# A transformer block on one core: the V products of two token blocks moved ahead of the first q and k products

## The chip, the core and the metric

The kernel runs on one core of a Trainium2 chip. PE is TensorE (matmuls and transposes), DVE is VectorE, ACT is ScalarE, POOL is GpSimd, and SP only issues DMAs here. PEld is the loading of a matmul's stationary operand. The metric is the device time of one execution in microseconds (us).

## The reference

The input is x, 2048 tokens of 512 numbers, all float32. It is normalized (mean 0, variance 1 over the 512, epsilon 1e-5). The result feeds two branches whose product is added to x:

```python
xn = layernorm(x)
q, k, v = split(xn @ wqkv)            # 32 heads of 16
s = concat(softmax(q @ k.T / 4) @ v) @ wo
g = silu(gelu(xn @ w1 + b1) @ w2 + b2)   # 1376 hidden
out = x + s * g
```

## The kernel before

**Precision.** A matmul operand is split in two parts: a high part, rounded on ACT, and a low part, the rest, computed on DVE or POOL (`split`, L86 and L87, for the normalized x; `w_split`, L294 and L295, for weights). A product then is three matmuls: high by high, high by low and low by high (`mm3`, L92).

**Blocks and chunks.** The tokens are worked in 16 blocks of 128, and four blocks make a chunk of 512. `xh` and `xl` hold the transposed high and low parts of a chunk.

**The first stage.** `load_x` fetches a block (L405). `ln` works on four blocks: statistics and their aggregate on DVE (L414, L415), one root for all four (L419 to L424: five small DVE operations with a square root on ACT, L420, between the first two), then four norms (L428). `turn` transposes a block on PE (L437) and splits it. `q_first` makes q and k of the first two head groups for a chunk: 24 matmuls of 512 columns (L455). Its `evac` copies the two results on ACT (L370), rounds them (L374), takes the low parts on POOL (L375), and SP stores the four tiles in DRAM (L380, L381). `v_tile` makes V of one block: 12 matmuls (L92), copied out on ACT (L387). V's own weights come in four pieces (L469), whose high parts are rounded on ACT (L511) and whose low parts are made on POOL (`wv_low`, L502). `pool_after(t)` is a one-element POOL operation that reads the norm of block t, so POOL does nothing that follows it before that norm is done. `keep_warm` issues small matmuls whose result nobody reads (L487).

On PE the first stage goes: warm-up matmuls, transposes of chunk 0, `q_first(0)`, transposes of chunk 1, V of block 0, `q_first(1)`, transposes of chunk 2, V of block 1, `q_first(2)`, transposes of chunk 3, V of block 2, `q_first(3)`, V of block 3.

**What follows.** When chunk 3 is transposed, the first stage's memory is given up. SP then issues `load_qs(0)`, six loads of q rows from DRAM (L146), and `load_k(0, ...)`, six loads of k rows of the first 512 tokens (L121); these come behind the stores of `q_first(2)` in SP's queue. The next stage is a list of products with 64 rows on each half of the PE array ("row tiles" 0 and 1): first V of blocks 4 to 15, four blocks at a time (`quad`, L583), then the feed-forward branch and the remaining q and k. Between these products, one after about five, stand the scans: a matmul of q and k rows (`s_mm`, L193) whose row maximum DVE takes (`s_max`, L199). The first scan stands behind the first four matmuls of the first quad. It needs the q and k rows of row tile 0, the second scan those of row tile 1. Later stages compute the scores again, with exponentials and V, and the output product.

**What sets the order.** The schedule is manual: every engine executes its instructions in the order in which the code issues them, and semaphores hold an instruction until what it reads is there. Nothing behind a held instruction of an engine is executed before it.

Of the kernel before, what the change touches and what calls it, by code (L numbers as in the profile page):

```python
# [8 lines left out]
F32 = mybir.dt.float32  # L9
F32R = mybir.dt.float32r  # L10
AF = mybir.ActivationFunctionType
# [5 lines left out]
P = 128  # L17
# [32 lines left out]
XB = 6  # L50
# [4 lines left out]
def fused(ctx: ExitStack, tc: tile.TileContext, x, wqk, wv, wo, w1, b1, w2, b2, out):  # L55
# [333 lines left out]
    with ExitStack() as s1:  # L389
# [19 lines left out]
        mv = wp.tile([P, NT, 2], F32, name="mv")  # L409
        ve = wp.tile([P, 5, NT], F32, name="ve")  # L410

        def moments(t):
            st = w1k.tile([P, 6], F32, name="st")
            nc.vector.bn_stats(st, xs[t])  # L414
            nc.vector.bn_aggr(mv[:, t, :], st)  # L415

        def rstd(t0, t1):
            v = ve[:, :, t0:t1]
            nc.vector.tensor_scalar(v[:, 0], mv[:, t0:t1, 1], EPS, None, op0=OP.add)  # L419
            nc.scalar.activation(v[:, 1], v[:, 0], AF.Sqrt)  # L420
            nc.vector.reciprocal(v[:, 2], v[:, 1])
            nc.vector.scalar_tensor_tensor(v[:, 3], v[:, 2], -0.5, v[:, 2], op0=OP.mult, op1=OP.mult)
            nc.vector.tensor_mul(v[:, 3], v[:, 3], v[:, 0])
# [9 lines left out]
        def turn(t):  # L433
            pt = a_tile((P, KT, P))
            xn = xns.pop(t)
            for k in range(KT):
                nc.tensor.transpose(pt[:, k, :], xn[:, k * P:(k + 1) * P], ident)  # L437
            c, ts = t // NCH, slice(t % NCH * P, t % NCH * P + P)
            split(xh[c][:, :, ts], xl[c][:, :, ts], pt)
# [5 lines left out]
                mm3(pv, (xh[c][:, k, ts], xl[c][:, k, ts]), (wv_h[:, k], wv_l[:, k]), k == 0, k == KT - 1)  # L445
            v_out(t, pv)

        def q_first(c):
            pq = {}
            for n, (i, j) in enumerate(((0, 0), (0, 1), (1, 0))):  # L450
                for g in range(2):
                    if n == 0:
                        pq["q", g, c] = a_tile((P, CH))
                    for k in range(KT):
                        nc.tensor.matmul(pq["q", g, c], W1[g][i][:, k * P:(k + 1) * P], (xh, xl)[j][c][:, k],  # L455
                                         start=n == 0 and k == 0, stop=n == 2 and k == KT - 1)
            evac(list(pq), pq)

        for t in range(4):
            load_x(t, (nc.sync, nc.scalar)[t % 2])  # L460
        warm = wp.tile([1, 2], F32, name="warm")
        nc.vector.memset(warm, 1.0)
        nc.scalar.activation(warm[:, 1:], warm[:, :1], AF.Sqrt)
        for g in range(2):
            W1[g] = w_new(wqk[:, g], 2, "raw1")
        for t in range(4, 6):
            load_x(t)
        for k in range(KT):
            nc.sync.dma_start(wv_r[:, k], wv[:, k])  # L469
        for t in range(6, XB):  # L470
# [14 lines left out]
        def keep_warm(n):  # L485
            for _ in range(n):
                nc.tensor.matmul(pw[:, :P], ident, ident, start=True, stop=True)  # L487

        keep_warm(25)
        def ln(t, n):  # L490
            for i in range(t, t + n):
                moments(i)
            rstd(t, t + n)
            for i in range(t, t + n):
                norm(i)

        ln(0, NCH)
        def pool_after(t):
            nc.gpsimd.tensor_sub(warm[:, :1], xns[t][:1, :1], xns[t][:1, :1])

        def wv_low(k):
            nc.gpsimd.tensor_sub(wv_l[:, k], wv_r[:, k], wv_h[:, k].bitcast(F32))  # L502

        pool_after(NCH - 1)
        for g in range(2):
            W1[g] = w_split(W1[g], "w1", 4)
        for t in range(NCH):
            turn(t)
        keep_warm(3)
        for k in range(KT):  # L510
            nc.scalar.activation(wv_h[:, k], wv_r[:, k], AF.Copy)  # L511
        for k in range(KT - 2):
            wv_low(k)
        ln(NCH, NCH)
        consts()
        pool_after(2 * NCH - 1)
        for k in range(KT - 2, KT):
            wv_low(k)
        q_first(0)
        for c in range(1, NCH):  # L520
            for t in range(NCH * c, NCH * c + NCH):
                turn(t)
            if c < NCH - 1:
                ln(NCH * c + NCH, NCH)
            else:
                nc.scalar.activation(warm[:, 1:], warm[:, :1], AF.Gelu_apprx_tanh)
                break
# [553 lines left out]
```

## Time and profile before

| | us |
|---|---|
| timed runs, median of 3 | 1547.04 (1546.8 to 1547.23) |
| span of the profiled execution | 1544.6 |
| PE busy in it | 1538.4 (100%) |
| DVE busy | 1419.2 (92%) |
| ACT busy | 1212.4 (78%) |
| POOL busy | 375.8 (24%) |

The profile shows one execution, whose span runs from the first to the last instruction; the timed runs lie 2.4 us above it. PE's busy time is modelled with matmuls that overlap, so 100% says that PE always has a matmul under way and not that it is at its peak. Times in rows count from the span's start. In a row such as `9.13 1.11 PE L437 ... x8 [0.22 <-DVE xn L428]` a group of 8 instructions starts at 9.13 and takes 1.11 us to the end of the last, and PE sat idle for 0.22 us before it until DVE's L428 was done. An fp32 transpose or warm-up matmul leaves two records. SPq is SP's queue, PEldq PE's sequencer, which goes ahead of the array and waits on semaphores.

### The profile page before, as it was taken

Reading aid. Unit: us, or ns where it says so; the run is one execution under the profiler, and the core shown is the slowest. Engines: PE = TensorE matmul, PEld = TensorE weight load, DVE = VectorE, ACT = ScalarE, POOL = GpSimd, SP = SyncE. Lnnn points to the kernel's source line nnn. Section 1 sums busy time; section 2 is a strip of 40 time slices with the busy share of each in tenths; the row PEclk is TensorE's granted clock in tenths of the full one; section 3 lists DMA queues with packets and bytes.
Section 4 is the critical chain, followed back from the end, with each engine's and each line's share of the span. In section 5 each row is a group of like instructions: output and inputs, shape, how many; then the busy total and the mean of one; then the engine's idle time right before and its main releaser. Section 6 shows DMA issues by size and latency. Waiting matters only on the chain.

```text
span 1544.6 us, 31302 instructions
## 1 busy us (share of the span) xinstructions
PE 1538.4 (100%) x12230; PEld 922.5 (60%) x12230; DVE 1419.2 (92%) x2294; ACT 1212.4 (78%) x1881; POOL 375.8 (24%) x386
## 2 busy tenths in 40 slices
PE   9999999999999999999999999999999999999998
PEld 8899999999995444444444444444444444444456
DVE  7799999999998999999999999999999999999945
ACT  4333433333339999999999999999999999999994
POOL 4235575756741011001000100100010000000153
PEclk9999999999999999999999999999999999999999
DMA  6615443455422112112411411411051111110162
GB/s 212 155 58 145 124 143 108 120 161 136 141 90 66 39 45 61 33 37 51 75 28 33 71 33 41 60 44 29 21 84 29 32 32 30 41 32 20 50 217 100
DMA packets 78227, 116.83 MB, mean 76 GB/s; under 512 B 28132, under 2 KB 28388, under 8 KB 76904
## 3 DMA queue, kind: packets, MB, share of 16 engines
q1 hardware_dynamic: 73596, 99.80, 23.1%
q0 software_dynamic: 4000, 14.45, 5.0%
q8 instruction: 96, 1.57, 0.4%
q10 hardware_dynamic: 484, 0.60, 0.1%
q14 instruction: 51, 0.42, 0.1%
HBM read 84.35 MB, written 25.97 MB: 71 GB/s over the span
## 4 chain that ended last, share of the span: by engine, by line
PE 99%; DVE 1%; DMA 0%; issue 0%; ACT 0%; DVEq 0%
PE pv L787 33%; PE ps L193 22%; PE ps L583 13%; PE two L716 8%; PE sp L583 5%; PE ps L716 4%; PE pst L716 4%; PE pst L583 3%; PE pv L583 2%; PE ps L916 2%; PE ps L92 1%; PE ps L455 1%; PE pst L92 0%; DVE st L414 0%; PE two L92 0%; DMA xt<-in_x 0%
## 5 line engine op out<-in xcount | busy, mean ns | idle before, releaser
L199 DVE TENSOR_REDUCE mx<-ps 128x2 f32<-128x512 f32 x2048 | 1318.0, 687 | 68.5 <-PE ps L193 18.3
L787 PE MATMUL pv<-slot,vsb 128*32 128x512 f32 x4096 | 543.4, 604 | 0.0
L721 ACT ACTIVATE slot<-two 128x1024 f32<-128x1024 f32 x511 | 520.5, 1019 | 0.0
L193 PEld LDWEIGHTS ps<-kt,slot 48*128 48x128 f32 x1356 | 212.2, 184 | 290.2 <-DVE mx L199 278.4
L193 PE MATMUL ps<-kt,slot 48*128 48x256 f32 (+1 forms) x1356 | 376.3, 366 | 0.0
L719 ACT ACTIVATE slot<-ps 128x512 f32<-128x512 f32 x515 | 307.5, 598 | 16.7 <-PE ps L716 7.2
L719 ACT ACTIVATE slot<-pst 128x512 f32<-128x512 f32 x511 | 309.9, 606 | 0.0
L583 PE MATMUL ps<-slot,w1h 64*128 64x512 f32 x1088 | 225.4, 392 | 0.0
L193 PE MATMUL ps<-kt,qz 48*128 48x512 f32 x512 | 202.2, 395 | 0.0
L716 PE MATMUL two<-qt,kt 50*128 50x512 f32 x766 | 197.5, 395 | 0.3 <-DVE gt L643 0.3
L716 PE MATMUL ps<-qt,kt 50*128 50x512 f32 x387 | 189.7, 492 | 0.0
L193 PEld LDWEIGHTS ps<-slot,slot 48*128 48x128 f32 x590 | 92.8, 184 | 124.0 <-DVE mx L199 118.2
L193 PE MATMUL ps<-slot,slot 48*128 48x256 f32 (+1 forms) x590 | 165.8, 366 | 0.0
L787 PEld LDWEIGHTS pv<-slot,vsb 128*32 128x32 f32 x4096 | 81.5, 108 | 131.9 <-issue 124.4
L583 PEld LDWEIGHTS ps<-slot,w1h 64*128 64x128 f32 x1088 | 154.1, 185 | 9.8
L583 PE MATMUL ps<-slot,w1l 64*128 64x512 f32 x544 | 157.0, 392 | 0.0
L716 PE MATMUL pst<-qt,kt 50*128 50x512 f32 x383 | 155.7, 406 | 0.0
L375 POOL TENSOR_TENSOR hl<-hg,hh 128x512 fp32r<-128x512 f32 x76 | 96.7, 1295 | 158.2 <-ACT hh L374 109.3
L368 ACT ACTIVATE hg<-ps,b_sb 128x512 f32<-128x512 f32 x44 | 27.9, 684 | 133.0 <-PE ps L583 121.7
L716 PEld LDWEIGHTS two<-qt,kt 50*128 50x128 f32 x766 | 114.5, 186 | 1.1 <-DVE gt L643 0.7
L246 POOL CAST mh<-nt 128x32 fp32r<-128x32 f32 x19 | 4.0, 209 | 375.7 <-DVE nt L244 322.8
L193 PEld LDWEIGHTS ps<-kt,qz 48*128 48x128 f32 x512 | 93.7, 183 | 1.0 <-DVE mx L199 0.7
(197 smaller groups left out, 1974.6 us busy)
## 6 DMA issues: line engine op xcount, KB each, us to landing
raw<-in_w SPq DMA_DIRECT2D x88, 256.0 KB
qk_h<-hh SPq DMA_DIRECT2D x32, 256.0 KB
qk_l<-hl SPq DMA_DIRECT2D x32, 256.0 KB
qt<-qk_h SPq DMA_DIRECT2D x128, 64.0 KB
slot<-qk_h SPq DMA_DIRECT2D x92, 64.0 KB
g_d<-gt POOLq DMA_DIRECT2D x16, 256.0 KB, 3.3
qt<-qk_l SPq DMA_DIRECT2D x64, 64.0 KB
dn<-den_d SPq DMA_DIRECT2D x32, 128.0 KB
```

Source lines behind the costliest of these rows:

```text
L92: nc.tensor.matmul(ps, lhs[a], rhs[b], start=first and n == 0, stop=last and n == 2)
L193: return nc.tensor.matmul(ps[:, c0:c0 + w], QS[u][r, p, qi * P:(qi + 1) * P], kts[u // NCH % KB][p][r, k0:k0 + w], start=True, stop=True).ins
L199: nc.vector.tensor_reduce(MX[u][:, 2 * p:2 * p + 2, qi, ki][:, heads, parts], ps.rearrange("p (n c) -> p n c", c=HC), axis=AX.X, op=OP.max)
L368: nc.scalar.activation(raw, ph.pop(u), AF.Gelu_apprx_tanh, bias=b1_sb[:, u[2]:u[2] + 1])
L375: nc.gpsimd.tensor_sub(hl, raw, hh.bitcast(F32))
L455: nc.tensor.matmul(pq["q", g, c], W1[g][i][:, k * P:(k + 1) * P], (xh, xl)[j][c][:, k], start=n == 0 and k == 0, stop=n == 2 and k == KT - 1)
L583: i = nc.tensor.matmul(ps, lhs[r], rhs[r], start=first, stop=last).ins
L716: nc.tensor.matmul(ps, kts[g % KB][p][r, k * P:(k + 1) * P], QT[u][r, p, :], start=True, stop=True)
L719: nc.scalar.activation(PT[u, k][:, 2 * p + a, :], ps, AF.Exp, scale=SCALE)
L721: nc.scalar.activation(PT[u, k][:, :2], TP["two"], AF.Exp, scale=SCALE)
L787: nc.tensor.matmul(PV[u][32 * j:32 * j + 32, :], vsb[:, k, h:h + 32], PT[u, k][:, j, :], start=(k == 0), stop=(k == NT - 1))
L916: HALF[0] = nc.tensor.matmul(PW[i][0], OTS[i, k][x][r], (wo_h, wo_l)[y][r, k], start=k == 0 and side == 0 and n == 0, stop=k == KT - 1 and ...
```

## The change

Six things change in the first stage.

- Block 0 is fetched in two halves by SP's and ACT's queues, block 1 by SP, block 2 by ACT, block 3 by SP. The V weights come ahead of the q and k weights, with block 3 behind their second piece.
- Blocks 0 and 1 get a square root of their own, and so do blocks 2 and 3. The root adds epsilon on ACT (`eps` is a small tile), so DVE has four small operations after it and none before.
- ACT rounds three pieces of the V weights ahead of the split of block 0, and the fourth ahead of the split of block 1. POOL makes the low parts of two pieces behind the norm of block 1 and of two behind the norm of block 3, and only then those of the q and k weights.
- The V products of blocks 0 and 1 are made ahead of `q_first(0)`, term by term (`v_term`), with the transposes of blocks 2 and 3 between them.
- The V products of blocks 2 and 3 take the places that those of blocks 0 and 1 had. Nothing stands any more between the transposes of chunk 3, `q_first(3)` and the first quad.
- The transposes of chunk 3 stand inside `q_first(2)`, ahead of its last four matmuls. The load of the Gelu table (`warm`, last line) comes behind the evacuation of `q_first(2)`. There are 15 warm-up matmuls instead of 28.

```diff
+        def root(t0, t1):
+            nc.scalar.activation(ve[:, 1, t0:t1], mv[:, t0:t1, 1], AF.Sqrt, bias=eps)
         def rstd(t0, t1):
-            nc.vector.tensor_scalar(v[:, 0], mv[:, t0:t1, 1], EPS, None, op0=OP.add)
-            nc.scalar.activation(v[:, 1], v[:, 0], AF.Sqrt)
...
+        def v_term(t, n):
+            i, j = ((0, 0), (1, 0), (0, 1))[n]
+            if n == 0:
+                VP[t] = a_tile((P, D))
+            c, ts = t // NCH, slice(t % NCH * P, t % NCH * P + P)
+            for k in range(KT):
+                nc.tensor.matmul(VP[t], (xh, xl)[i][c][:, k, ts], (wv_h, wv_l)[j][:, k],
+                                 start=n == 0 and k == 0, stop=n == 2 and k == KT - 1)
+            if n == 2:
+                v_out(t, VP.pop(t))
+
-        def q_first(c):
+        def q_first(c, mid=()):
...
+                    if n == 2 and g == 1:
+                        for t in mid:
+                            turn(t)
...
-        for t in range(4):
-            load_x(t, (nc.sync, nc.scalar)[t % 2])
+        xs[0] = w1k.tile([P, D], F32, name="xt", bufs=XB)
+        for eng, r in ((nc.sync, slice(0, P // 2)), (nc.scalar, slice(P // 2, P))):
+            eng.dma_start(xs[0][r], x[r, :])
+        load_x(1)
+        load_x(2, nc.scalar)
...
+        for k in range(KT):
+            if k == 2:
+                load_x(3)
+            nc.sync.dma_start(wv_r[:, k], wv[:, k])
         for g in range(2):
             W1[g] = w_new(wqk[:, g], 2, "raw1")
...
-        keep_warm(25)
+        keep_warm(15)
...
+        moments(0)
+        moments(1)
+        root(0, 2)
+        stats(2)
+        rstd(0, 2)
+        norm(0)
+        norm(1)
+        aggr(2)
+        moments(3)
+        for k in range(KT - 1):
+            wv_high(k)
+        pool_after(1)
+        turn(0)
+        wv_high(KT - 1)
+        turn(1)
+        root(2, 4)
+        rstd(2, 4)
+        norm(2)
+        norm(3)
+        for k in range(2):
+            wv_low(k)
+        pool_after(3)
+        for k in range(2, KT):
+            wv_low(k)
         for g in range(2):
             W1[g] = w_split(W1[g], "w1", 4)
+        v_term(0, 0)
+        v_term(1, 0)
+        v_term(0, 1)
+        turn(2)
+        v_term(1, 1)
+        turn(3)
+        v_term(0, 2)
+        v_term(1, 2)
         ln(NCH, NCH)
...
-        for c in range(1, NCH):
+        for c in range(1, NCH - 1):
             for t in range(NCH * c, NCH * c + NCH):
                 turn(t)
...
-            v_tile(c - 1)
-            q_first(c)
+            ln(NCH * c + NCH, NCH)
+            v_tile(c + 1)
+            q_first(c, range(NT - NCH, NT) if c == NCH - 2 else ())
+        nc.scalar.activation(warm[:, 1:], warm[:, :1], AF.Gelu_apprx_tanh)
...
     load_k(0, c0=CH, n=S - 2 * CH)
-    v_tile(NCH - 2)
     q_first(NCH - 1)
-    v_tile(NCH - 1)
     load_k(0, c0=S - CH, n=CH)
```

The change shifts line numbers: transposes are L446, the early V products L465, `q_first` L480, warm-up matmuls L517, V weight roundings L533, low parts L536, quads L633.

How instructions move on PE at the start. Before (`slot_97` and `slot_101` are `xh` and `xl` of chunk 0, `kt_113` holds the V weights' parts, `w1h` and `w1l` those of q and k):

```order
L487 MATMUL pv<-ident 128x128 x25
L437 MATMUL ps<-ident,xn 128x128 x8
L437 MATMUL sp<-ident,xn 128x128 x8
L487 MATMUL pv<-ident 128x128 x3
L455 MATMUL pst<-slot_97,w1h 128x512 x4
L455 MATMUL ps<-slot_97,w1h 128x512 x4
L455 MATMUL pst<-slot_101,w1h 128x512 x4
```

With the change:

```order
L517 MATMUL pv<-ident 128x128 x15
L446 MATMUL ps<-ident,xn 128x128 x8
L465 MATMUL sp<-kt_113,slot_97 128x512 x8
L465 MATMUL sp<-kt_113,slot_101 128x512 x4
L446 MATMUL pst<-ident,xn 128x128 x4
L465 MATMUL sp<-kt_113,slot_101 128x512 x4
L446 MATMUL ps<-ident,xn 128x128 x4
L465 MATMUL sp<-kt_113,slot_97 128x512 x8
L480 MATMUL ps<-slot_97,w1h 128x512 x8
```

24 V matmuls and the transposes of blocks 2 and 3 now stand between the first two blocks' transposes and `q_first(0)`.

On ACT at the start, before (L420 is the root, L294 rounds the q and k weights, L86 is a block's split, L511 rounds the V weights):

```order
L420 ACTIVATE ve<-ve 128x4
L294 ACTIVATE w1h<-raw_135 128x512
L294 ACTIVATE w1h<-raw_137 128x512
L86 ACTIVATE slot_97<-ps 128x4x128 x2
L86 ACTIVATE slot_97<-sp 128x4x128 x2
L511 ACTIVATE kt_113<-wv_r 128x512 x4
```

With the change (L426 is the root, L533 rounds the V weights):

```order
L426 ACTIVATE ve<-mv,eps 128x2
L533 ACTIVATE kt_113<-wv_r 128x512 x3
L86 ACTIVATE slot_97<-ps 128x4x128
L533 ACTIVATE kt_113<-wv_r 128x512
L86 ACTIVATE slot_97<-ps 128x4x128
L426 ACTIVATE ve<-mv,eps 128x2
L294 ACTIVATE w1h<-raw_142 128x512
```

Three weight roundings now stand ahead of block 0's split.

On PE at the third `q_first` (chunk 2 is `slot_99` and `slot_103`, chunk 3 `slot_100` and `slot_104`), before; V of block 2 follows with 12 matmuls of L92, of which the first rows are shown, then the last `q_first`, V of block 3 with 12 more, four quad matmuls and the first scan:

```order
L455 MATMUL ps<-slot_103,w1h 128x512 x8
L455 MATMUL ps<-slot_99,w1l 128x512 x8
L437 MATMUL sp<-ident,xn 128x128 x8
L437 MATMUL pst<-ident,xn 128x128 x4
L437 MATMUL ps<-ident,xn 128x128 x4
L92 MATMUL ps<-kt_113,slot_97 128x512 x2
L92 MATMUL ps<-kt_113,slot_101 128x512
```

With the change, from there to the first scan L193:

```order
L480 MATMUL sp<-slot_99,w1l 128x512 x4
L446 MATMUL pst<-ident,xn 128x128 x4
L446 MATMUL ps<-ident,xn 128x128 x12
L480 MATMUL sp<-slot_99,w1l 128x512 x4
L480 MATMUL sp<-slot_100,w1h 128x512 x8
L480 MATMUL sp<-slot_104,w1h 128x512 x8
L480 MATMUL sp<-slot_100,w1l 128x512 x8
L633 MATMUL pst<-kt_113,slot_98 128x512
L633 MATMUL pv<-kt_113,slot_98 128x512
L633 MATMUL pst<-kt_113,slot_98 128x512
L633 MATMUL pv<-kt_113,slot_98 128x512
L193 MATMUL ps<-kt_623,qz_632 128x512
```

Between the last matmul of the third `q_first` and the first scan there are now one `q_first` and four quad matmuls.

On SP at the same place nothing moves; with the change, as before, the rows read:

```order
L380 DMA qk_h<-hh 128x512
L381 DMA qk_l<-hl 128x512
L146 DMA qz_632<-qk_h 16x2x512
L146 DMA qz_632<-qk_l 16x2x512
L146 DMA qz_632<-qk_h 16x2x512 x2
L146 DMA qz_632<-qk_l 16x2x512
L146 DMA qz_632<-qk_h 16x2x512
L121 DMA kt_623<-qk_h 16x2x512 x2
L121 DMA kt_623<-qk_l 16x2x512
L121 DMA kt_623<-qk_h 16x2x512 x2
L121 DMA kt_623<-qk_l 16x2x512
```

The first two rows are the last stores of the third `q_first`, the others the twelve loads for the first scans.

More of the change, by code (lines that the diff above doesn't have):

```diff
@@ L457, in q_first @@
             evac(list(pq), pq)
-        for t in range(4):
-            load_x(t, (nc.sync, nc.scalar)[t % 2])
+        xs[0] = w1k.tile([P, D], F32, name="xt", bufs=XB)
[3 more added lines that the diff above has]
+        load_x(2, nc.scalar)
         warm = wp.tile([1, 2], F32, name="warm")
+        eps = wp.tile([P, 1], F32, name="eps")
         nc.vector.memset(warm, 1.0)
+        nc.vector.memset(eps, EPS)
         nc.scalar.activation(warm[:, 1:], warm[:, :1], AF.Sqrt)
+        for k in range(KT):
+            if k == 2:
+                load_x(3)
+            nc.sync.dma_start(wv_r[:, k], wv[:, k])
         for g in range(2):
             W1[g] = w_new(wqk[:, g], 2, "raw1")
[L466 to L470, printed above, removed]
+        for t in range(4, XB):
             load_x(t)
@@ L492, in ln @@
                 moments(i)
+            root(t, t + n)
             rstd(t, t + n)
```

37 lines of the change are left out of this document (14 added, 23 removed).

## The prediction

> **What bounds the kernel now.** I read the page's chain of waits first. PE carries nearly all of it, so a microsecond gained or lost on PE moves the end, unless a later stage gives it back.
>
> ```profile
> span 1544.6 us, 31302 instructions
> PE 99%; DVE 1%; DMA 0%; issue 0%; ACT 0%; DVEq 0%
> ```
>
> Second, the chain of waits in order of time for the first 60 us (start, length, what), where all edited code lies:
>
> ```profile
> 0.74 3.13 DMA xt<-in_x
> ...
> 20.11 2.79 PE pst L92 x12
> ...
> 28.50 0.44 PE ps L437 x4
> ...
> 33.01 5.60 PE ps L455 x24
> 38.61 0.89 PE sp L437 x8
> 39.51 0.46 PE pst L437 x4
> 40.42 2.75 PE ps L92 x12
> ...
> 48.76 2.79 PE sp L92 x12
> ```
>
> From 18 us on PE is the chain without a break: one V product of a block (L92) costs 2.8 us, one `q_first` (L455) 5.60 us, or 0.233 a matmul, one block's transposes (L437) 0.45. Before that the chain is a load and DVE. So the change has two places: the start, where PE has little to do, and 38 to 52 us, where the V products that it takes away stood ahead of the first scan (L193).
>
> **The start.** The timeline (start, busy, engine and line, idle time before it in brackets), then busy time in stretches (PE, PEld, DVE, ACT, POOL, clock, DMA share, GB/s):
>
> ```profile
> 1.36 7.54 PE L487 MATMUL pv<-ident 128*128 128x128 f32 x50 [1.36 <-POOL ident masks.py:199]
> 4.72 0.66 DVE L414 BATCH_NORM_STATS2 st<-xt 128x6 f32<-128x512 f32 x1
> 7.72 0.18 DVE L421 RECIPROCAL ve<-ve 128x4 f32<-128x4 f32 x1 [0.27 <-ACT ve L420]
> 7.86 1.33 ACT L294 ACTIVATE w1h<-raw 128x512 fp32r<-128x512 f32 x2 [0.18 <-DMA raw<-in_wqk]
> 8.53 1.92 DVE L428 TENSOR_SCALAR xn<-xt,mv,ve 128x512 f32<-128x512 f32 x4
> 9.13 1.11 PE L437 MATMUL ps<-ident,xn 128*128 128x128 f32 x8 [0.22 <-DVE xn L428]
> 9.82 1.08 ACT L86 ACTIVATE slot<-ps 128x512 fp32r<-128x512 f32 x2 [0.63 <-PE ps L437]
> 10.45 1.29 DVE L87 TENSOR_TENSOR slot<-ps,slot 128x512 fp32r<-128x512 f32 x2
> 11.74 2.21 ACT L511 ACTIVATE kt<-wv_r 128x512 fp32r<-128x512 f32 x4
> 11.94 1.19 PE L455 MATMUL pst<-slot,w1h 128*128 128x512 f32 x4
> 13.24 2.55 POOL L502 TENSOR_TENSOR kt<-wv_r,kt 128x512 fp32r<-128x512 f32 x2
> 18.11 1.09 PE L437 MATMUL ps<-ident,xn 128*128 128x128 f32 x8 [0.32 <-DVE xn L428]
> ```
>
> ```profile
> 2.00:4.00 2.00, 2.00 (x11) 2.00 (x11) 0.11 (x1) 1.15 (x2) 0.44 (x2) 1.00 0.97 330
> 4.00:6.00 2.00, 2.00 (x16) 2.00 (x15) 1.93 (x5) 0.00 (x0) 0.00 (x0) 1.00 0.97 313
> 6.00:8.00 2.00, 2.00 (x21) 2.00 (x20) 1.59 (x7) 0.34 (x2) 0.00 (x0) 1.00 0.96 329
> ```
>
> Block 0 lands at 3.87 with block 1's 0.26 MB interleaved. Cut over two queues it has that much less beside it: 0.26 MB at 330 GB/s is 0.8 us, so about 3.2 (bounds 2.9 and 3.87). Blocks 1 and 2 follow interleaved, 0.52 MB or 1.6 us: 4.8. Statistics and aggregate of block 1 take 0.83 (3.89 to 4.72); the root on ACT hides behind block 2's statistics; the reciprocal comes at 6.4, the first norm 0.81 behind it (7.72 to 8.53), the first transpose 0.60 behind that (8.53 to 9.13): 7.8, which is 1.3 earlier.
>
> But the V products need all four pieces of the V weights, and ACT works in order: three roundings stand ahead of block 0's split. In load order the third piece ends at 1.83 MB, the fourth at 2.10. The rows move 1.95 MB by 8 us, so the third has been moved at 7.65; yet the fifth 0.26 MB of before, moved by 6.05, released L294 only at 7.86, 1.8 later. With that lag the third piece is there at 9.45, without it at 8.0. By the later: rounding (2.21 / 4, 0.6) to 10.1, split of block 0 (1.08 / 2) to 10.65, fourth rounding to 11.2, split of block 1 to 11.75. The first V matmul runs at 10.65, block 1's first four end at 12.8, the next four at 13.7. DVE takes block 1's low part to 12.5 and only then the second root: reciprocal, 0.81, two norms of 0.54 to 14.4. POOL's `pool_after(3)` waits for the last norm, and two low weight parts (2.55) stand behind it: 17.0. The last five V matmuls wait for those, so the first `q_first` starts at 18.3. It started at 11.94; with 24 V matmuls (5.6) ahead it would break even at 17.54. That is 0.75 lost. The second block's norms, which were late (24 matmuls from 11.94 end at 17.54, the transposes came at 18.11), are in time now: 0.55 back. Net 0.2 lost with the lag, about 1.0 gained without. I take a gain of 0.4. The bounds: 2.9 gained if nothing but the first transpose is waited for (7.8, 16 transposes of 0.11 and 5.6 end at 15.2), 1.2 lost if each hand-over is later by a microsecond.
>
> At nothing: ten warm-up matmuls fewer (PE has no work there), one DVE operation fewer per root (0.2, DVE is ahead of PE until the last block), x4 and x5 loaded last (their statistics now come after 17 us), the Gelu table load behind the third evacuation (ACT idle there). Without their cover the table would cost 1.3.
>
> **The third block and the first scan.** The V products of blocks 0 and 1 now lie at the start, so everything up to block 8's transposes (28.50) stands 5.6 − 0.4 = 5.2 later; I go on on the old clock and add 5.2 at the end.
>
> ```profile
> 36.48 0.17 DVE L419 TENSOR_SCALAR ve<-mv 128x4 f32<-128x4 f32 x1
> 37.73 1.92 DVE L428 TENSOR_SCALAR xn<-xt,mv,ve 128x512 f32<-128x512 f32 x4
> 38.71 0.60 ACT L370 ACTIVATE hg<-ps 128x512 f32<-128x512 f32 x1 [0.34 <-PE ps L455]
> 42.64 0.38 SPq L381 DMA_DIRECT2D qk_l<-hl  x1
> 43.20 0.32 SPq L146 DMA_DIRECT2D qz<-qk_h  x1
> 48.24 0.42 SPq L121 DMA_DIRECT2D kt<-qk_l  x1
> L193 PEldq EVENT_SEMAPHORE  x1: 2000/2000/2000, 48.2 to 48.2; - x1
> L193 PEldq EVENT_SEMAPHORE  x2: 51/51/51, 50.5 to 51.2; - x2
> 52.07 0.39 PE L193 MATMUL ps<-kt,qz 48*128 48x512 f32 x1
> 52.52 0.40 PE L193 MATMUL ps<-kt,qz 48*128 48x512 f32 x1
> 52.49 22.98 DVE L199 TENSOR_REDUCE mx<-ps 128x2 f32<-128x512 f32 x33 [9.14 <-PE ps L193]
> ```
>
> Read here what the first scan waits for. SP issues in order: the last store of the third `q_first` at 42.64, then twelve loads of q and k rows from 43.20 to 48.24. PE's weight sequencer stood at the first scan from 48.2 for 2000 ns, to 50.2, and came to the second row tile's semaphore at 51.2; the scans ran at 52.07 and 52.52. So before, the loads arrived just as PE did, because four blocks' transposes (1.8), two V products (5.6) and a `q_first` (5.6) lay between the third `q_first` and the quads. Of these only the `q_first` is left.
>
> In the change PE reaches the transposes inside `q_first` at 33.01 + 20 × 0.233 = 37.67; the norm comes at 37.53 (0.2 sooner), its transpose 0.60 later: 0.5 waited, and 0.2 more as three norms of 0.54 pace transposes of 0.45. So the third `q_first` ends at 38.61 + 1.8 + 0.7 = 41.1. ACT makes the four splits first, so its second evacuation starts 0.4 after that end, not 0.1: 41.5. From there the chain is unchanged: 4.5 to the first load (38.71 to 43.20), 7.0 and 8.0 to the two arrivals (50.2 and 51.2), 0.6 to the matmul (51.5 to 52.07): scans at 53.6 and 54.6. PE is free far sooner: its last `q_first` waits 0.45 for the two banks that ACT is still emptying, then 5.6 and four quad matmuls (0.5): 47.65. **PE idles for about 5.9 us** in front of L193, and the quads are queued behind it in order; nothing else can run. DVE's second reduce starts at 55.0 instead of 53.2 (52.49 + 0.69): 1.8 on the old clock, with 5.2 **7.0 us later**. From then on L199 runs back to back (33 in 22.98), so the delay isn't given back. Bounds: 4.5 with the start's full gain of 2.9, 8.6 with its loss of 1.2.
>
> **The clock.** Does a pause of 5.9 us cost more than itself? The only long pause is the end:
>
> ```profile
> 1540.40 0.28 PE L92 MATMUL two<-wo_h,slot 128*128 128x256 f32 x1
> 1540.00:1544.60 4.60, 0.68 (x6) 0.47 (x5) 1.47 (x4) 0.00 (x0) 0.00 (x0) 0.97 0.35 122
> ```
>
> A mean clock of 0.97 over 4.6 us is half speed for the last 0.25 or so: it fell about 3.7 us after the last matmul. And 11 matmul records in 2 to 4 us, 16 in 4 to 6 and 21 in 6 to 8 show half speed at the start until about 5, some 3.6 us after 1.36, though the clock column reads 1.00 there. A pause of 5.9 is longer than 3.7, so I let the clock fall; 3.6 us at half speed lose 1.8. Bounds 0 (it holds) and 3.6 (it takes twice as long). [...]
>
> **The sum.** 7.0 + 1.8 = 8.8 on a span of 1544.6; the timed runs lie 2.4 above the span, and I add it to their median: 1547.04 + 8.8 = **1555.8**, 0.57% slower.
>
> **The rivals.**
> 1. The pause comes, the clock holds: 7.0, 1554.0. For it: only one fall is seen, after 3.7 us, and a shorter pause (a faster store chain) would not reach it. Chance 0.33.
> 2. The start gains in full, 2.9 instead of 0.4: weights there without lag and POOL not the last. Against it: L294's wait, and POOL's two parts behind the fourth norm. The pause remains, since the store chain shifts with PE: 4.5, 1551.5; with the fall 1553.3. Chance 0.07.
> 3. The other side: the first scan doesn't wait, because its rows arrive 5.9 us sooner than 43.20's chain says; from a pause under 1 us on this decides. Then the start, the norms' 0.7 and the banks' 0.45 are all: between 1.15 − 2.9 and 1.15 − 0.4, so 1545.3 to 1547.8. For it: fewer DMAs compete by then. Against it: SP issues these loads behind the stores in both orders, twelve at 0.46 each. Chance 0.07, nearly all within 0.2%.
> That the change misses its own aim, V products filling the start, is in the forecast already: they wait for weights, low parts and norms about as long as PE idled.
>
> **How the numbers follow.** The forecast has 0.50 (its own range 1554 to 1558), rivals 0.33, 0.07 and 0.07, and 0.03 is for a cost above 11. The range 1551.5 to 1558 takes in rivals 1 and 2 and the bounds of the clock. Within 0.2% (3.1 us, what a measurement can tell from no change) lies most of rival 3, 0.06; faster 0.03; slower 0.91.
>
> **What would show it.** First transposes near 7.8; first V matmul near 10.7, held by ACT's roundings; the first `q_first` near 18.3, behind POOL's low parts; L193 first at 59, after a PE pause of 5 to 6.5 us that a semaphore wait of PE's sequencer spans; a clock under 1 behind it; DVE's L199 starting 7 us later. Wrong would be: no pause in front of L193, a `q_first` before 16, or a later stage in which the shift shrinks.

## The result and the profile after

The median went from 1547.04 us (1546.8 to 1547.38) to **1556.32 us** (1554.84 to 1557.34): a ratio of 1.0059, with a 95% interval of 1.0048 to 1.007, or 9.3 us slower. The forecast was 1555.8. The profiled execution of the change is the longest of its five, 1557.34 with a span of 1555.5, so 10.9 above the span of before.

Pieces of the chain of waits in the first 60 us, in order of time (start, length, what):

```profile
3.69 5.96 DMA wv_r<-in_wv
10.83 4.61 PE sp L465 x12
17.25 1.85 PE sp L465 x8
19.10 5.60 PE ps L480 x24
26.45 2.76 PE ps L92 x12
...
47.88 5.88 PE sp L480 x24
56.13 3.71 DMA kt<-qk_h
```

Before, PE was this chain without a break from 18 us on. Now a load of k rows (`kt<-qk_h`) lies on it for 3.71 us, behind the last `q_first` (L480, 5.88 us). The V weights have taken the place of block 0 as the load that the start hangs on.

**The start.** The timeline (start, busy, engine and line, idle time before it), and busy time in stretches (PE, PEld, DVE, ACT, POOL, clock, DMA share, GB/s):

```profile
4.37 0.69 DVE L416 BATCH_NORM_STATS2 st<-xt 128x6 f32<-128x512 f32 x1 [3.47 <-DMA xt<-in_x]
...
8.99 1.11 PE L446 MATMUL ps<-ident,xn 128*128 128x128 f32 x8 [2.61 <-DVE xn L437]
...
9.66 0.63 ACT L533 ACTIVATE kt<-wv_r 128x512 fp32r<-128x512 f32 x1 [0.86 <-DMA wv_r<-in_wv]
...
10.83 4.61 PE L465 MATMUL sp<-kt,slot 128*128 128x512 f32 x12 [0.73 <-ACT slot L86]
...
14.50 2.52 POOL L536 TENSOR_TENSOR kt<-wv_r,kt 128x512 fp32r<-128x512 f32 x2
...
18.94 3.89 PE L480 MATMUL ps<-slot,w1h 128*128 128x512 f32 x16
...
24.54 1.03 PE L446 MATMUL sp<-ident,xn 128*128 128x128 f32 x8
```

```profile
10.00:12.00 2.00, 1.27 (x4) 0.96 (x4) 1.11 (x4) 2.00 (x6) 2.00 (x2) 0.79 1.05 398
12.00:14.00 2.00, 2.00 (x6) 1.61 (x5) 1.86 (x7) 1.01 (x2) 0.21 (x1) 0.50 0.50 186
14.00:16.00 2.00, 2.00 (x11) 1.59 (x11) 0.21 (x1) 0.09 (x1) 1.65 (x3) 0.86 0.62 168
```

In this trace the transposes left one record each (64 in L446, four for each of 16 blocks) and the warm-up matmuls two (30 in L517 for 15), so `x8` in L446 is two blocks.

The first V matmul runs at 10.83, behind the third V weight piece and the split of block 0. Then the clock drops to half (0.50 from 12 to 14 us), and 12 matmuls take 4.61 us where the same number took 2.8 before. The transposes of the second chunk (the forecast calls it the second block) start at 24.54. They started at 18.11, and 5.6 us of V products are new ahead of them: in this execution the start lost 0.83 us.

**The first scan.** Timeline and stretches again:

```profile
47.88 4.00 PE L480 MATMUL sp<-slot,w1h 128*128 128x512 f32 x16 [0.34 <-ACT hg L370]
...
51.53 0.32 SPq L381 DMA_DIRECT2D qk_l<-hl  x1
...
52.02 0.32 SPq L146 DMA_DIRECT2D qz<-qk_h  x1
...
57.07 0.42 SPq L121 DMA_DIRECT2D kt<-qk_l  x1
...
59.95 0.76 PE L193 MATMUL ps<-kt,qz 48*128 48x512 f32 x1 [5.55 <-DMA kt<-qk_h]
...
60.75 0.69 DVE L199 TENSOR_REDUCE mx<-ps 128x2 f32<-128x512 f32 x1 [12.36 <-PE ps L193]
```

```profile
54.00:60.00 6.00, 0.45 (x6) 0.08 (x2) 0.00 (x0) 1.48 (x3) 2.48 (x2) 0.91 0.87 155
60.00:66.00 6.00, 6.00 (x30) 5.17 (x32) 2.90 (x5) 0.00 (x0) 0.00 (x0) 0.52 1.07 241
66.00:72.00 6.00, 6.00 (x55) 5.69 (x53) 5.82 (x9) 0.00 (x0) 0.00 (x0) 1.00 0.84 234
```

PE stands still for 5.55 us until the k rows arrive, with the quads queued behind the scan; the 0.45 us in which it is busy in the first stretch are nearly all quad matmuls ahead of it. In the trace the clock is at half (0.50) from 58.95 to 65.77; in the middle stretch DVE is busy for 2.90 of 6 us, and only in the third does the stage run as it should.

**Nothing is given back.** The scans' rows in the view that groups by line, before and then with the change. This row holds the scans on later k tiles; its two times are the starts of the first and the last:

```profile
L193 PE MATMUL ps<-kt,slot x1356: 274/385/502, 590.8 to 1464.6; 48*128 48x512 f32 x101, 48*128 48x256 f32 x93
```

```profile
L193 PE MATMUL ps<-kt,slot x1356: 274/385/502, 601.3 to 1475.1; 48*128 48x512 f32 x101, 48*128 48x256 f32 x93
```

They are 10.5 us later at 590.8 and 10.5 at 1464.6. Of this 7.9 is the first scan (52.07 to 59.95), and 2.6 comes while the clock is low. I use these two readings for every run below: the first scan, and the first row of this group. Before, they lie 538.7 apart (52.07 to 590.8).

### The profile page after: what moved, and what is told of

Same layout as the page of the kernel before. It is cut to its first block, busy times and chain, and to the rows that moved or that the text cites. A ratio compares the mean times of both kernels' runs of the same rounds, so it can differ in the third digit from the quotient of the medians.

```text
span 1555.5 us, 31252 instructions
## 1 busy us (share of the span) xinstructions
PE 1540.1 (99%) x12204; PEld 925.7 (60%) x12204; DVE 1418.3 (91%) x2295; ACT 1212.8 (78%) x1882; POOL 376.2 (24%) x386
## 4 chain that ended last, share of the span: by engine, by line
PE 98%; DMA 1%; DVE 1%; ACT 0%; SPq 0%; issue 0%; ACTq 0%
PE pv L837 33%; PE ps L193 22%; PE ps L633 13%; PE two L766 8%; PE sp L633 5%; PE ps L766 4%; PE pst L766 4%; PE pst L633 3%; PE pv L633 2%; PE ps L966 2%; PE ps L92 1%; PE sp L480 1%; PE ps L480 1%; PE sp L465 0%; DMA wv_r<-in_wv 0%; PE two L92 0%
## 5 line engine op out<-in xcount | busy, mean ns | idle before, releaser
L193 PEld LDWEIGHTS ps<-kt,slot 48*128 48x128 f32 x1356 | 212.4, 184 | 290.0 <-DVE mx L199 278.4
L193 PE MATMUL ps<-kt,slot 48*128 48x256 f32 (+1 forms) x1356 | 376.7, 366 | 0.0
L633 PE MATMUL ps<-slot,w1h 64*128 64x512 f32 x1088 | 226.1, 392 | 0.0
L193 PE MATMUL ps<-kt,qz 48*128 48x512 f32 x512 | 203.4, 397 | 5.5 <-DMA kt<-qk_h 5.5
L193 PEld LDWEIGHTS ps<-slot,slot 48*128 48x128 f32 x590 | 92.9, 184 | 123.9 <-DVE mx L199 118.2
L193 PE MATMUL ps<-slot,slot 48*128 48x256 f32 (+1 forms) x590 | 165.7, 365 | 0.0
L633 PEld LDWEIGHTS ps<-slot,w1h 64*128 64x128 f32 x1088 | 155.7, 185 | 8.4
L633 PE MATMUL ps<-slot,w1l 64*128 64x512 f32 x544 | 157.6, 392 | 0.0
L193 PEld LDWEIGHTS ps<-kt,qz 48*128 48x128 f32 x512 | 94.4, 184 | 7.0 <-issue 5.9
```

What stands on the lines that cost most here:

```text
L193: return nc.tensor.matmul(ps[:, c0:c0 + w], QS[u][r, p, qi * P:(qi + 1) * P], kts[u // NCH % KB][p][r, k0:k0 + w], start=True, stop=True).ins
L633: i = nc.tensor.matmul(ps, lhs[r], rhs[r], start=first, stop=last).ins
```

## The experiments

My theory was that of the forecast: V products and transposes that stood behind the third `q_first` covered the chain of stores and loads that the first scan waits for; the change put them ahead of it, and a clock that falls in the pause adds to that. Rivals were that the start is what costs, that DMA traffic is, or that the scan stage is bound by PE, so that the place of the pause doesn't matter.

| run | median (range), us | ratio to before, interval | first scan | group's first row | between |
|---|---|---|---|---|---|
| before | 1547.04 (1546.8 to 1547.38) | | 52.07 | 590.8 | 538.7 |
| change | 1556.32 (1554.84 to 1557.34) | 1.0059 (1.0048 to 1.007) | 59.95 | 601.3 | 541.4 |
| e1 | 1553.46 (1552.64 to 1554.88) | 1.0043 (1.0031 to 1.0056) | 58.03 | 596.9 | 538.9 |
| e2 | 1554.92 (1553.87 to 1555.22) | 1.0051 (1.0038 to 1.0063) | 57.58 | 597.7 | 540.1 |
| e3 | 1555.06 (1554.06 to 1555.69) | 1.0052 (1.0039 to 1.0064) | 58.90 | 599.4 | 540.5 |
| e4 | 1554.58 (1554.03 to 1555.56) | 1.005 (1.0037 to 1.0064) | 59.79 | 598.6 | 538.8 |
| e5 | 1555.23 (1554.76 to 1555.63) | 1.0051 (1.0039 to 1.0064) | 57.12 | 598.9 | 541.8 |
| e6 | 1551.79 (1551.37 to 1552.44) | 1.003 (1.0018 to 1.0041) | 55.74 | 596.4 | 540.7 |
| e7 | 1549.33 (1549.11 to 1550.79) | 1.0017 (1.0008 to 1.0026) | 54.68 | 593.2 | 538.5 |
| e8 | 1547.03 (1546.26 to 1547.5) | 0.9998 (0.9989 to 1.0007) | 52.04 | 590.6 | 538.6 |
| e9 | 1547.19 (1546.1 to 1547.6) | 1.0001 (0.9993 to 1.001) | 52.59 | 591.3 | 538.7 |
| e10 | 1550.88 (1549.84 to 1552.46) | 1.0027 (1.0016 to 1.0037) | 51.21 | 596.8 | 545.6 |
| e11 | 1548.81 (1548.55 to 1549.44) | 1.0013 (1.0004 to 1.0022) | 49.54 | 593.1 | 543.6 |
| e12 | 1555.37 (1554.12 to 1557.7) | 1.0058 (1.0045 to 1.007) | 57.92 | 598.6 | 540.7 |

The last three columns are of one profiled execution each, and a start of the same code moves by half a microsecond from one to another (transposes of the second chunk at 23.24 in e6, 23.73 in e5), and by 1.5 where the clock falls in it (24.75 in e4). The kernel before ran between 1546.8 and 1547.16 in median beside them.

### e1: the cover put back

The change's start is kept; the V products of blocks 2 and 3 return to their old places around the last `q_first`.

```diff
-            v_tile(c + 1)
             q_first(c, range(NT - NCH, NT) if c == NCH - 2 else ())
...
+    v_tile(NCH - 2)
     q_first(NCH - 1)
+    v_tile(NCH - 1)
```

> The changed kernel with the V products of blocks 2 and 3 at their old places (block 2 between the transposes' chunk and the last q_first, block 3 behind it); start and transposes inside the third q_first as in the change. Theory 'cover' (PE reaches the first scan 5.6 us of work too early, and the load chain behind the third q_first sets the scan): the pause of 5.5 us before L193 shrinks below 0.7, the clock doesn't fall there, and 1.0 at the start plus 0.7 at the transposes stay: 1548 to 1549.5. Rival 'late chain' (the loads themselves are late, because ACT makes four splits ahead of the evacuation): the scan comes as late as with the change and the time stays above 1553.

As expected, the pause and the fall of the clock behind it are gone in the profiled execution, the fastest of the five: PE runs from 46.14 us into the first scan without a break, the clock is 1.00 from 54 to 72 us, and the time between the two readings is 538.9, that of before. The time itself was missed by more than 3 us. It lies where the rival put it, but the rival's cause, late loads, isn't there. The chain in order of time and three stretches say where the time is:

```profile
23.56 0.60 ACT hg L370
24.16 1.04 ACT hh L374 x2
25.20 1.96 ACT slot L86 x4
27.16 0.04 issue
27.20 5.88 PE ps L480 x24
```

```profile
23.50:27.20 3.70, 1.77 (x17) 1.53 (x15) 1.48 (x3) 3.59 (x7) 2.44 (x2) 1.00 0.94 314
33.10:36.80 3.70, 2.00 (x16) 1.68 (x16) 2.88 (x7) 3.59 (x7) 2.44 (x2) 1.00 0.67 228
36.80:42.87 6.07, 4.94 (x21) 3.70 (x21) 5.43 (x16) 0.30 (x1) 0.07 (x1) 1.00 0.44 120
```

ACT empties two banks, rounds them and makes four splits before the next `q_first` can start: 3.6 us, in which PE is busy 1.77 and then 2.00 of 3.70. The V product of each turn of the loop had filled that. So the V products covered two different waits, ACT's in the loop and the loads' at its end, and the two at the loop's end can't be given to the start without opening one of them. PE stood still for 1.93, 1.70 and 1.13 us in these stretches, 4.8 in all (the third for norms that come late). That is most of the 6.0 by which the first scan is later than in the kernel before; the theory that all the cost is in the last wait falls here.

### e2: the change's tail alone

The start is that of before. V of blocks 0 and 1 stands ahead of the second `q_first`, V of blocks 2 and 3 ahead of the third, and the last transposes inside the third, as in the change.

```diff
-        def q_first(c):
+        def q_first(c, mid=()):
...
-            v_tile(c - 1)
-            q_first(c)
+            for t in range(2 * c - 2, 2 * c):
+                v_tile(t)
+            q_first(c, range(NT - NCH, NT) if c == NCH - 2 else ())
...
-    v_tile(NCH - 2)
     q_first(NCH - 1)
-    v_tile(NCH - 1)
```

> The kernel before with its old start, but V of blocks 0 and 1 ahead of the second q_first, V of blocks 2 and 3 ahead of the third, and the transposes of chunk 3 inside the third q_first, so that only one q_first lies between it and the quads. Theory 'cover': the pause of 5 to 6 us and the fall of the clock come without any change at the start: 1553.5 to 1556.5. Rival 'start' (most of the 9.3 us is lost where V weights and the clock hold the first V products): under 1550.

1554.92, as expected. With the old start PE pauses for 4.45 us, and 7.9 of the 9.3 us are there:

```profile
57.58 0.76 PE L193 MATMUL ps<-kt,qz 48*128 48x512 f32 x1 [4.45 <-DMA kt<-qk_h]
```

The start's part is the rest, about 1.4, though the ranges of the two overlap a little.

### e3: work put in the pause

```diff
-FILL0 = 2
+FILL0 = 12
```

The first scan then stands behind 24 quad matmuls instead of 4.

> The changed kernel with 24 quad matmuls instead of 4 ahead of the first scan (FILL0 12 for 2). Theory 'cover': 20 matmuls in pairs of 0.233 us fill 2.3 us of the pause, which falls from 5.5 to about 3.2; the first scan comes at the same time. [...] Rival 'late chain' says the same of the scan's time and nothing of the sum.

PE does 20 matmuls in the pause, which shrinks to 2.36 us. The first scan comes 1.05 earlier than with the change, 0.15 of it by its start; its loads take 7.0 us from the first issue to the scan, where they took 7.9. The first scan in the timeline, and two stretches behind it:

```profile
58.90 0.47 PE L193 MATMUL ps<-kt,qz 48*128 48x512 f32 x1 [2.36 <-DMA kt<-qk_h]
```

```profile
60.00:62.00 2.00, 2.00 (x15) 2.00 (x13) 1.48 (x3) 0.00 (x0) 0.00 (x0) 0.65 0.95 312
62.00:64.00 2.00, 2.00 (x12) 2.00 (x10) 1.06 (x2) 0.00 (x0) 0.00 (x0) 0.50 1.08 203
```

Yet 540.5 us lie between the readings, and 540.1 in e2, which did no such work but had as long a low clock (3.4 us in both). PE work taken out of the scan stage gains nothing: there DVE sets the pace, and the end follows the first scan. The clock fell here too, after a pause of only 2.36 us.

### e4: the pause kept warm

```diff
     q_first(NCH - 1)
+    idle = ps_m.tile([P, CH], F32, name="ps")
+    for _ in range(20):
+        nc.tensor.matmul(idle, wv_h[:, 0, :P], xh[0][:, 0], start=True, stop=True)
```

> The changed kernel with 20 matmuls of 512 columns whose result nobody reads between the last q_first and the quads (4.7 us). If half speed after the pause is part of the loss, the first scan comes at the same time (59.9 us) and the time falls by the 2.4 us that the profile shows between the first and the sixth reduce: about 1554, and the runs scatter less. If the half speed is covered by something else, the time stays at 1556.3.

```profile
59.79 0.47 PE L193 MATMUL ps<-kt,qz 48*128 48x512 f32 x1 [0.50 <-DMA kt<-qk_l]
```

With 4.7 us of matmuls more in front of it the first scan stays where it was (59.79), the clock stays up (1.00 from 54 to 66 us), and 538.8 lie between the readings as in the kernel before. So the low clock behind the pause is worth 541.4 − 538.8 = 2.6 us in the profiled executions and 1.7 in the medians, whose intervals overlap. Pause and clock are two costs, and the pause is the larger.

### e5: the k rows by another queue

```diff
-    load_k(0, c0=0, n=CH)
+    load_k(0, eng=nc.scalar, c0=0, n=CH)
```

> The changed kernel with the six loads of k rows for the first scan issued from ACT's queue beside SP's six loads of q rows, instead of behind them. If the chain from the stores to the scan is bound by SP's issuing (twelve at 0.46 us), the last of them is issued 2.7 us sooner and the first scan comes 2 to 2.7 us sooner: 1553 to 1554.5. If it is bound by the transfers (the DMA share is 0.87 in the pause), the scan moves by less than 0.8 us: 1555.5 to 1556.5.

Rows of both queues and of ACT from the timeline:

```profile
50.07 0.82 ACTq L121 DMA_DIRECT2D kt<-qk_h  x2
...
52.08 1.22 SPq L146 DMA_DIRECT2D qz<-qk_h  x2
...
54.52 0.44 ACTq L121 DMA_DIRECT2D kt<-qk_l  x1
55.06 1.09 ACT L370 ACTIVATE hg<-sp 128x512 f32<-128x512 f32 x2 [5.01 <-DMA kt<-qk_l]
55.53 0.30 SPq L146 DMA_DIRECT2D qz<-qk_l  x1
```

The result lies between the two expectations. With two queues the k loads start 4.7 us earlier (50.07 against 54.79) and the first scan comes at 57.12 instead of 59.95. But SP issued nothing between 53.3 and 55.53, and ACT's evacuations waited behind its loads. The issue in a row on one queue is a part of the chain: of the 2.8 us by which the first scan is earlier, 0.8 is the start of this execution (second chunk's transposes at 23.73 instead of 24.54), and 2.0 the second queue. What holds SP up stays open.

### e6: the last transposes behind the third `q_first`

```diff
-            q_first(c, range(NT - NCH, NT) if c == NCH - 2 else ())
+            q_first(c)
+        for t in range(NT - NCH, NT):
+            turn(t)
```

> The changed kernel with the transposes of chunk 3 behind the third q_first instead of inside it. Theory 'ahead of the third q_first's end counts, behind it is free': its end and the stores come 2.5 to 3 us sooner (transposes 1.8, their wait 0.7, four splits on ACT ahead of the evacuation), so does the first scan, and the splits that PE then waits for lie inside the pause: 1553 to 1554.2. Rival: the last q_first waits for the splits, the load chain isn't what counts: no gain or a loss, 1556 or more.

More than expected: 4.5 us off the time. From PE's timeline:

```profile
23.24 1.04 PE L446 MATMUL sp<-ident,xn 128*128 128x128 f32 x8
...
55.74 0.47 PE L193 MATMUL ps<-kt,qz 48*128 48x512 f32 x1 [1.88 <-DMA kt<-qk_l]
```

The first scan is 4.21 earlier than with the change. The first row shows that 1.30 of this is the start of this execution (24.54 there), whose clock did not fall (1.00 from 8 to 16 us). The other 2.9 is what the transposes cost inside `q_first`. The first load goes out at 48.23 instead of 52.02, which is 2.5 earlier when the start is taken off: the forecast's 1.8 of work and 0.7 of waits for norms. Its third term, 0.4 for ACT's splits ahead of the second evacuation, isn't there: from the end of the third `q_first` to the first load it is 4.5 us with the change and 4.6 here. The last 0.4 lies between that load and the scan, 7.5 us instead of 7.9.

The pause is down to 1.88. PE now also waits ahead of the last `q_first`, for ACT's splits of chunk 3:

```profile
47.33 4.00 PE L480 MATMUL sp<-slot,w1h 128*128 128x512 f32 x16 [1.98 <-ACT slot L86]
```

That wait costs nothing, since PE is still at the first scan 1.88 us before its rows are there. This run and e4 are the plainest tests of the mechanism: **what stands ahead of the stores delays the first scan; what stands behind them doesn't, as long as PE still waits for the loads.**

### e7: one V product across the line

The kernel before, with V of block 2 ahead of the third `q_first` instead of behind it.

```diff
             v_tile(c - 1)
+            if c == NCH - 2:
+                v_tile(c)
             q_first(c)
...
-    v_tile(NCH - 2)
     q_first(NCH - 1)
```

> The kernel before with one V product, that of block 2, moved from behind the transposes of chunk 3 to a place ahead of the third q_first. Nothing else is changed, and PE has the same work. Theory 'ahead counts, behind is free': the third q_first's end, the stores and the loads come 2.8 us later, and the first scan by 2.8 less the 0.3 that PE spends at the quads' start before: 1549.3 to 1550, a pause of 2 to 2.8 us before L193, no fall of the clock. Rival 'the start and the clock carry the loss': within 1 us of before.

The last `q_first` and the first scan in PE's timeline:

```profile
45.56 1.20 PE L455 MATMUL ps<-slot,w1h 128*128 128x512 f32 x4 [1.99 <-ACT slot L86]
...
54.68 0.39 PE L193 MATMUL ps<-kt,qz 48*128 48x512 f32 x1
```

2.8 us of work moved across the third `q_first`, no work added: the first scan comes 2.6 later (0.5 of it its start) and the end 2.2. The size is the expected one, but the pause that was expected in front of L193 isn't there. PE stands still for 1.99 us one `q_first` earlier, until ACT has made the splits of chunk 3, which V of block 2 covered before. It is the wait that e1 found in the loop. The loads went out later as well (the first at 46.19 instead of 43.20), and PE's sequencer waited at L193 for the rows of the two row tiles until 52.9 and 54.05, while PE reached the quads at 54.12. The loads alone would have held the scans nearly as long; this run can't tell the two apart. Four of its eleven runs lie at 1550.5 to 1550.8 and the others at 1549.1 to 1549.6. The profiled one is of the lower group, and its clock held (mean 1.000); what the four lost stays open.

### e8: the root alone

The kernel before with the change's root: epsilon is added on ACT, and four small DVE operations remain of five.

```diff
-            nc.vector.tensor_scalar(v[:, 0], mv[:, t0:t1, 1], EPS, None, op0=OP.add)
-            nc.scalar.activation(v[:, 1], v[:, 0], AF.Sqrt)
+            var = mv[:, t0:t1, 1]
+            nc.scalar.activation(v[:, 1], var, AF.Sqrt, bias=eps)
             nc.vector.reciprocal(v[:, 2], v[:, 1])
-            nc.vector.scalar_tensor_tensor(v[:, 3], v[:, 2], -0.5, v[:, 2], op0=OP.mult, op1=OP.mult)
-            nc.vector.tensor_mul(v[:, 3], v[:, 3], v[:, 0])
+            nc.vector.scalar_tensor_tensor(v[:, 3], var, EPS, v[:, 2], op0=OP.add, op1=OP.mult)
+            nc.vector.scalar_tensor_tensor(v[:, 3], v[:, 3], -0.5, v[:, 2], op0=OP.mult, op1=OP.mult)
...
```

> The kernel before with the change's root alone (epsilon added by ACT, four small DVE operations instead of five). At the start and at the second chunk's transposes PE waits for norms, so each operation saved there (0.2 us) counts: 0.2 to 0.4 us faster than before, 1546.6 to 1546.8. If PE's waits there are ended by something else, no difference.

No difference, where a small gain was expected: 0.2 us on DVE at the start does not show in a measurement of this kernel.

### e9, e10, e11: can the first scan come earlier than before?

If the first scan sets the end, the kernel before should gain from an earlier one. e9 issues the four stores of the third `q_first` behind the 12 loads of the first scan. e10 spreads V of block 3 through the first quad, three matmuls at a time (`v_late`, called in each of its four runs). e11 does both.

```diff
+            hold[0] = c == NCH - 2
             q_first(c)
...
     load_k(0, c0=0, n=CH)
+    hold[0] = False
+    stores()
```

```diff
-    v_tile(NCH - 1)
...
             hooks = {}
+            if n == 0:
+                hooks[6] = [lambda: v_late(i)]
```

> The kernel before, with the four stores of the third q_first issued on SP behind the 12 loads of the first scan instead of ahead of them, so that the loads can start at about 41 us instead of 43.2 and the last lands near 49.0 instead of 51.21. Theory (TensorE's work up to the quads at 51.49 and the loads end within half a microsecond of each other in the kernel before, so that neither alone brings the first scan forward): no difference, 1546.8 to 1547.3. Rival (the loads alone set the first scan): 1545.0.

> The kernel before, with the V product of token block 3 (12 matmuls, 2.9 us) taken from ahead of the quads and spread through the first quad, three matmuls at a time. Theory (the loads still land at about 51.2): TensorE reaches the quads 2.9 us earlier, at 48.6, and stops there for some 2 us before the first scan; no difference, 1546.5 to 1547.5. Rival (TensorE's work ahead alone sets the first scan): 1544.2 to 1545. Second rival (the scan stage is bound by TensorE, so that 2.9 us of matmuls among the scans cost as much there): as before in any case.

> Both of the last two edits on the kernel before. Theory (the time of the first scan sets the end, microsecond for microsecond, and TensorE has room among the scans): the first scan comes at about 50 instead of 52.07 and the end by as much: 1544.8 to 1545.3. Rival (the scan stage is bound by TensorE): 1546.8 to 1547.2, since the sum of its work is the same.

e9 came as expected, no difference. The loads are issued some 1 to 2 us earlier (the first at 41.01 instead of 43.20, the last at 47.19 instead of 48.24), but PE is not there sooner. e10 and e11 fell out in a way that no theory had. First scans of e10 and e11:

```profile
51.21 0.47 PE L193 MATMUL ps<-kt,qz 48*128 48x512 f32 x1 [1.36 <-DMA kt<-qk_h]
```

```profile
49.54 0.39 PE L193 MATMUL ps<-kt,qz 48*128 48x512 f32 x1
```

In e11 the first scan is 2.5 us early, where about 2 was expected, and the end is 2.0 late. A stretch of the scan stage of before, then of e11:

```profile
54.00:58.00 4.00, 4.00 (x37) 3.88 (x36) 3.89 (x6) 0.00 (x0) 0.00 (x0) 1.00 1.04 144
```

```profile
54.00:58.00 4.00, 4.00 (x30) 3.02 (x28) 2.83 (x5) 0.00 (x0) 0.00 (x0) 1.00 1.09 294
```

PE is full in both, and DVE falls from 3.89 to 2.83 of 4 us. The 12 matmuls cost 2.8 us ahead of the quads and 543.6 − 538.7 = 4.9 among the scans. So the theory holds only with a limit: the scan stage has DVE and PE both near full. Taking PE work out of it wins nothing (e3), putting some in costs more than the work itself. e10 adds a pause (1.36 us) and a low clock (0.68 from 54 to 58 us) to that. PE's timeline of e11 shows where most of the 4.9 lies, here at the second of the four pieces:

```profile
55.57 0.39 PE L594 MATMUL pst<-kt,slot 64*128 64x512 f32 x1
55.89 0.97 PE L92 MATMUL ps<-kt,slot 128*128 128x512 f32 x3
56.79 0.50 PE L594 MATMUL pst<-kt,slot 64*128 64x512 f32 x1
```

From the last product of a row tile ahead of a piece to the first behind it 1.2 us pass, where two such products otherwise follow each other in 0.23. This piece of three matmuls so costs 1.0 instead of 0.7, and the four, taken as alike, 4.0, an estimate. Where the other 0.9 lies was not settled.

No version beat the kernel before.

### e12: a warmer start

```diff
-        keep_warm(15)
+        keep_warm(25)
...
         turn(1)
+        keep_warm(8)
```

> The kernel with the change, with 25 instead of 15 dummy matmuls ahead of the first transpose and 8 more behind the second block's transposes, so that TensorE is busier ahead of the fall of its clock at 11 us. Theory (that fall stretched the first V products and is most of the start's loss): no fall there, and 0.7 to 1.0 us faster than with the change alone, 1555.3 to 1555.7. Rival (the start is set by the weights' low parts on GpSimd and not by TensorE's clock): 1556.1 to 1556.5.

Rows of PE's timeline:
```profile
11.03 3.02 PE L465 MATMUL sp<-kt,slot 128*128 128x512 f32 x12
...
23.15 1.03 PE L446 MATMUL sp<-ident,xn 128*128 128x128 f32 x8
```

In this execution the clock stays up at the start (1.00 from 8 to 20 us): 12 V matmuls take 3.02 us instead of 4.61, and the second chunk's transposes come at 23.15, 1.39 earlier than with the change. In time the run is inconclusive: the median is 0.95 below the change's, but the ranges overlap wholly. Nor do the dummy matmuls have to be the reason. The change's own start, unaltered in e1, e5 and e6, had no fall either (transposes at 23.36, 23.73 and 23.24), while it fell in e3 and e4 (24.39 and 24.75). So the fall is there in three of six executions of that start, and costs about 1.

## Why the prediction was right

**The bound and the two places** were read rightly: no stage behind the first scan changed, and the shift is the same at 590.8 and at 1464.6.

**The first scan: right.** Behind the second chunk's transposes the forecast gave 35.5 us to the first scan (18.11 + 5.2 to 58.8), and the trace 35.4 (24.54 to 59.95). The pause was forecast at 5.9 and is 5.55. e2 shows that the change's tail alone makes the pause, and e4, e5 and e6 that the first scan waits for the loads behind the third `q_first`: matmuls put in front of it don't move it, a second queue brings it 2.0 forward, work taken from ahead of the stores 2.5 to 2.9. That the forecast is right to 0.1 is in part luck. The loads went out 0.4 earlier than forecast and took 0.3 longer; from the first load to the scan the runs with a pause and one queue took between 6.8 us (e2) and 7.9 (the change). The transposes and the waits for norms are borne out by e6; the 0.4 for ACT's splits is not.

**The start: the term was mis-sized, by 1.2.** The forecast took a gain of 0.4, the profiled execution lost 0.83. Two steps of it were off. Block 0's statistics were to start at 3.2 and started at 4.37, later than before (3.89), so the first transposes came at 8.99 and not at 7.8. That cost nothing, because V waited for its weights in any case: third rounding at 9.66 (forecast 9.45, by the lag that I chose to believe), first V matmul at 10.83 (10.65), POOL's low parts done at 17.02 (17.0). What cost was the clock, which the forecast let fall only in the pause. Without that fall the start is as forecast: 23.15 to 23.73 in e12, e1, e5 and e6, against 23.31.

**The clock behind the pause: right in kind, mis-sized.** Forecast 1.8, from 3.6 us at half speed; e4 puts it at 2.6 in the profiled execution, where half speed lasted 6.8 us, and at about 1.7 in the median. The step that failed is the threshold, my estimate from the one fall at the end of the trace of before: a pause had to reach some 3.7 us before the clock would fall. It fell after 2.36 us in e3, 1.88 in e6 and 1.36 in e10. So rival 1, the pause with a clock that holds, was given too much: in none of the six profiled executions with a bare pause in front of the first scan (change, e2, e5, e6, e10, e12) did it hold. Length alone doesn't decide: waits of 1.93 us (e1), 1.98 (e6) and 1.99 (e7) ahead of a `q_first` left the clock up.

**The sum.** 8.8 forecast, 9.3 in the median, 10.9 in the profiled execution, which had both falls, the longer one at the pause. It is near because the terms that carry it, V products and transposes moved ahead of the stores, were read from rows. That the median is within 0.5 is in part luck: with the start's 1.2 and a fall that costs 2.6 the forecast's terms come to 10.8, and the median is lower, probably because the falls are there only in part of the executions. Rival 2 (the start's full gain) fell with the weights' arrival; rival 3 with the pause.

## What to carry to other kernels

Work that looks like a delay in front of a stage can be the cover of a round trip through memory. Before moving it, find the store that the stage's first load waits for, and ask on which side of that store the work will stand: here 4.7 us of matmuls behind it were free, as long as PE still waited for the chain (e4: the scan at 59.79), and about 2.5 us of work and waits taken from ahead of it brought the stage 2.9 forward (e6). The gap that the work would fill elsewhere has to be priced with every wait that it uncovers at its old places: those for another engine's splits as well as those for a load (e1: 4.8 us in the loop, e7: 1.99). And a stage with two engines near full can lose more by an addition (4.9 in e11) than it wins by an earlier beginning (2.5).

## What the runs showed of the hardware that was not expected

- The clock fell behind pauses shorter than the 3.7 us between the last matmul and the fall at the end of the trace of before: 2.36 us (e3), 1.88 (e6) and 1.36 (e10). It also fell at the start of the change, where PE was idle for 2.61 and 0.73 us with 1.11 of transposes between. It did not fall in e1 (mean clock 1.000), where PE was busy 1.77 of 3.70 us and then 2.00 of 3.70, nor behind a wait of 1.99 in e7 (1.000).
- The falls lasted about 3.4 us at the starts of the change, e3 and e4 and at the pauses of e2, e3, e6 and e10, and about 6.8 at those of the change, e5 and e12. The start of the change had one in three of six executions: in the change, e3 and e4, and not in e1, e5 and e6. What sets the lengths was not shown.
- A load cut over two queues landed later: both halves of block 0 went out at 0.74, and the statistics waited for them until 4.37; the whole block had been there at 3.89 before. The loads behind it are ordered differently too, and the cut alone was not tried.
- The same 12 matmuls over all rows cost 2.8 us ahead of a stage with both PE and DVE near full (4.00 and 3.89 of 4 us before), and 4.9 within it (e11), by estimate 4.0 of that where they stand between products of the row tiles.
